# Windowed-attention scores in blocks of 32 queries by 96 keys, from the eleventh token tile on

## The chip, the cores and the metric

The kernel runs on one core of one Trainium2 chip. The metric is the device time of one execution in microseconds (us). The kernel before takes 512.82 us, the median of three runs (511.93 to 513.01).

## What is computed

For 8 sequences of 576 positions and 8 heads of width 64, each query attends to itself and to the 63 positions ahead of it. The result, 4608 tokens by 512 features in fp32, goes through a feed-forward block with a softmax gate and a layer norm.

```python
scores = (q @ k.T) / sqrt(64)
rel = pos[:, None] - pos[None, :]
scores = where((rel >= 0) & (rel < 64), scores, -1e9)
x = softmax(scores) @ v
h = x @ w_in
solu = h * softmax(h)
y = (layer_norm(solu) * g_ln) @ w_out
```

The queries of 32 neighbouring positions need 95 keys between them, those of 64 neighbours need 127.

## The kernel before

The 4608 tokens are cut into 36 tiles of 128, each two blocks of 64 queries of one sequence. One tile goes through these stages.

- `scores` (L445, matmul on L460): for each of 4 pairs of heads, each block of 64 queries (`half`) and each head of the pair (`r`), a matmul of 64 queries by 128 keys with the 64 features of the head as contraction. `r` picks the rows of the TensorE array and `half` its columns, so four such matmuls lie on four array tiles of 64x64. The result goes into a PSUM tile `pS`, where `r` is the outer index. A sequence's first block has no keys ahead of it, and its own keys are read twice. Each fp32 matmul stands in the trace as two records, each with a weight load of its own.
- `softmax` (L468): VectorE adds the mask and takes the maximum out of `pS` (L475, one operation per head, all 128 key columns), ScalarE takes the exponential (L480), GpSimd scales (L498).
- `cross` (L508) and `transposes` (L519): the probabilities are split into 16-bit halves by ScalarE (L512), transposed by DMA (L515, on SP's queue), and joined by VectorE into `PT` (L522).
- `values` (L552, matmul on L559): probabilities times values into `pO`, 32 matmuls of 64 columns a tile, on two array tiles of 128x64; `xH` (L573) and `xL` (L574) are its high and low parts.
- `moe_in` (L585, matmul on L603): 24 matmuls of 512 columns into the one PSUM tile `pH`. `moe_norm` reads `pH` by VectorE (L618), ScalarE (L620) and VectorE (L623), and the next tile's `moe_in` can write it only after L623.
- `moe_cross`, `moe_join` (L666, L669, L679, L683, L685): the normed row is transposed as above, into `yH` and `yL`.
- `moe_out` (L715, matmul on L737): 24 matmuls of 512 columns, and the result is stored.

A planner (`Plan`) writes out the order of every engine. Each step has a cost in ns, its reads and writes and a ring of buffers (`RINGS`; `pS` has 2), and `Plan.order` places the steps by due time and by the costs; the PE order itself is the order in which the steps are written down. The scores of one tile are two steps of cost 480. From the eighth tile on the tiles go in pairs: per pair TensorE runs `values` of two tiles, `scores` of two later tiles, then `moe_out`, `moe_in`, `moe_out`, `moe_in`. `T` (L297) hands out a tile: it makes a new one of the ring for each (tag, number).

Of the kernel before, what the change touches and what calls it, by code (L numbers as in the profile page):

```python
# [18 lines left out]

P = 128  # L20
WIN = 64
BIG = 3.0e38

EXP_HI = 122879.9921875
# [202 lines left out]
def tile_window_attention_solu_moe(  # L227
# [17 lines left out]
    nc = tc.nc  # L245
# [6 lines left out]
    D = P // 2  # L252
# [10 lines left out]
    ps_s = ctx.enter_context(tc.tile_pool(name="ps_s", bufs=1, space=bass.MemoryType.PSUM))  # L263
# [6 lines left out]

    band = const.tile([P, P + WIN], F32, name="band")
    nc.gpsimd.memset(band, 0.0)
    nc.gpsimd.affine_select(
        band, band, pattern=[[-1, P + WIN]], base=WIN, channel_multiplier=1,
        compare_op=ALU.is_ge, fill=NEG)
    nc.gpsimd.affine_select(
        band, band, pattern=[[1, P + WIN]], base=-1, channel_multiplier=-1,
        compare_op=ALU.is_ge, fill=NEG)
    masks = {}
    for first in (0, None, 1):  # L280
        t = masks[first] = const.tile([P, P], F32, name=f"mask{first}")
        nc.gpsimd.tensor_copy(t[:WIN], band[:WIN, :P])
        nc.gpsimd.tensor_copy(t[WIN:], band[WIN:, WIN:])
        if first is not None:
            nc.gpsimd.memset(t[first * WIN:(first + 1) * WIN, :WIN], NEG)

# [7 lines left out]

    plan = Plan(RINGS, NTILE, NW)

    def T(tag, n, shape, dtype=F32, pool=None):  # L297

        if (tag, n) not in plan.tiles:
            plan.tiles[tag, n] = (pool or sb).tile(  # L300
                shape, dtype, tag=tag, name=f"{tag}_{n}", bufs=RINGS[tag])
        return plan.tiles[tag, n]

    def first_of(t):

        return {0: 0, NBLK - 1: 1}.get(2 * t % NBLK)
# [4 lines left out]
    def W32(i):  # L311
        return T("w", i, [P, 2, 512])

    def WL(i):
        return T("w", NW + i, [P, 2, 512], F32R)
# [6 lines left out]
    def weight_block(i, src):  # L322
# [3 lines left out]
        def raw():  # L326
            return T("raw", i, [P, 2, 512, 2], I32)
# [79 lines left out]
    def Q(t):  # L407
        return QK(t)[:, :NPAIR * P].rearrange("d (p s) -> d p s", p=NPAIR)

    def K(t):  # L410
        return QK(t)[:, NPAIR * P:].rearrange("d (p s) -> d p s", p=NPAIR)
# [16 lines left out]
    def SS(t):  # L428
        return T("sS", t, [P, H, P])

    def PS(t, x=0):
        if (t, x) == (0, 1):
            return T("pH", NTILE, [P, 2, NPAIR, P], pool=ps_h)
        return T("pS", t, [P, 2, NPAIR, P], pool=ps_s)

    def S_key(t, x):
        return ("pH", NTILE) if (t, x) == (0, 1) else ("pS", t)
# [7 lines left out]
    def scores(t):  # L445
        first = first_of(t)

        def emit(ps=range(NPAIR)):
            q, k = Q(t), K(t)

            for p in ps:
                for half in range(2):
                    for r in range(2):
                        rs = slice(r * D, (r + 1) * D)
                        keys = k[rs, p, half * WIN:half * WIN + P]
                        if first == half:
                            a = k[rs, p, (half + 1) * WIN:(half + 2) * WIN]
                            keys = bass.AP(
                                tensor=a.tensor, offset=a.offset, ap=[a.ap[0], [0, 2], a.ap[1]])
                        nc.tensor.matmul(  # L460
                            PS(t, p // 2)[half * WIN:(half + 1) * WIN, r, p],
                            q[rs, p, half * WIN:(half + 1) * WIN], keys, start=True, stop=True)

        for x in range(2):
            plan.op("PE", 480, lambda x=x: emit((2 * x, 2 * x + 1)), [("qk", t)], [S_key(t, x)],
                    loose=t < LOOSE)

    def softmax(t):  # L468
        def cols(tag, h):
            return T(tag, t, [P, H], pool=st)[:, h:h + 1]  # L470

        mk = masks[first_of(t)]
        for h in range(H):

            plan.op("DVE", 211, lambda h=h: nc.vector.tensor_tensor_reduce(  # L475
                SS(t)[:, h], PS(t, h // 4)[:, h % 2, h // 2], mk, scale=-SCALE, scalar=BIG,
                op0=ALU.add, op1=ALU.min, accum_out=cols("nmx", h)),
# [283 lines left out]
    def attend(t):  # L761
        on(scores, t + AHEAD)
        on(softmax, t + AHEAD)
        on(cross, t + AHEAD)

    load(0, range(1))
    prep(0)
    scores(0)
    softmax(0)
    load(0, range(1, 2))  # L770
# [3 lines left out]
    transposes(0)  # L774
    values(0)
    scores(1)
    softmax(1)
    prep(3)
# [121 lines left out]
```

## Time and profile before

| what | before |
|---|---|
| median of the runs | 512.82 us (511.93 to 513.01) |
| span of the profiled execution | 510.9 us, first to last instruction; its own time is not listed apart from the runs |
| TensorE (PE) busy | 492.1 us, 96% of the span |
| VectorE (DVE), ScalarE (ACT), GpSimd (POOL) busy | 80%, 70%, 62% |
| score matmuls (L460) | 2 x 576 records, 6% of the chain that ended last |
| granted TensorE clock | full in all 40 slices of the span |

The median of the runs lies 1.9 us above the span, which is what stands around the first and the last instruction. Busy time says where an engine has work, not where it holds the others up; that is read from the chain of waits.

### The profile page before, as it was taken

The page shows a single profiled execution, that of the slowest core. Times are in us where ns is not written, and L with a number is a line of the kernel's source. Part 1 is how long each engine was busy: PE and PEld are TensorE (multiplying, and loading weights), DVE is VectorE, ACT ScalarE, POOL GpSimd, SP SyncE. Part 2 cuts the span into 40 slices and gives each one's busy share as a digit, 9 for nine tenths or more (in the row PEclk, how much of TensorE's full clock was granted, in tenths as well). Part 3 has the DMA queues.
Part 4 walks back from the last instruction along what each step waited for, and adds up shares of the span by engine and source line. Part 5 has one row for each costly group of instructions (what it writes and reads, how often), then busy time and mean ns, then how long its engine had stood idle before and what let it go on. Part 6 is the DMA issues. An engine that isn't in the chain of part 4 may idle for free.

```text
span 510.9 us, 11601 instructions
## 1 busy us (share of the span) xinstructions
PE 492.1 (96%) x4064; PEld 392.4 (77%) x4064; DVE 409.8 (80%) x1176; ACT 355.6 (70%) x960; POOL 314.5 (62%) x566
## 2 busy tenths in 40 slices
PE   2889999999999999999999999999999999999996
PEld 1445577888788888888888888888888888888885
DVE  5998997888796989787978898887878878977531
ACT  4589795868686777777776868686859586865331
POOL 4388467664757475758574858584848485936430
PEclk9999999999999999999999999999999999999999
DMA  8994446966889989898889797879897969764301
GB/s 321 412 410 177 116 120 119 234 156 147 173 219 148 234 164 229 171 223 163 229 151 243 143 250 145 250 141 247 132 244 144 267 117 222 124 131 103 83 21 43
DMA packets 150762, 94.09 MB, mean 184 GB/s; under 512 B 135088, under 2 KB 135344, under 8 KB 150320
## 3 DMA queue, kind: packets, MB, share of 16 engines
q1 hardware_dynamic: 150704, 93.35, 76.7%
q8 instruction: 32, 0.52, 0.5%
q14 instruction: 26, 0.21, 0.1%
HBM read 50.86 MB, written 9.44 MB: 118 GB/s over the span
## 4 chain that ended last, share of the span: by engine, by line
PE 85%; DVE 4%; ACT 2%; POOL 2%; DMA 2%; issue 0%; SPq 0%; ACTq 0%; DVEq 0%; POOLq 0%
PE pH L603 34%; PE pO L737 34%; PE pO L559 6%; PE pS L460 6%; PE pO L724 3%; PE pH L590 1%; DMA raw<-raw 1%; ACT sS L480 1%; POOL sS L498 1%; PE pS L700 1%; DVE e L623 1%; DVE mst L618 1%; DMA y<-ot 1%; ACT e L620 0%; DVE w L368 0%
## 5 line engine op out<-in xcount | busy, mean ns | idle before, releaser
L498 POOL TENSOR_SCALAR sS<-sS,rec 128x128 f32<-128x128 f32 x280 | 149.2, 554 | 10.8 <-PE pS L460 7.4
L480 ACT ACTIVATE sS<-sS,nmx 128x128 f32<-128x128 f32 x288 | 111.5, 389 | 1.5 <-DVE nmx L475 1.4
L737 PE MATMUL pO<-w_outH,yH 128*128 128x512 f32 x272 | 108.2, 398 | 0.0
L737 PE MATMUL pO<-w,yH 128*128 128x512 f32 x272 | 106.1, 390 | 0.0
L603 PE MATMUL pH<-w_inH,xH 128*128 128x512 f32 x264 | 103.7, 393 | 0.8 <-DVE mst L623 0.8
L603 PE MATMUL pH<-w,xH 128*128 128x512 f32 x264 | 101.8, 389 | 0.0
L737 PE MATMUL pO<-w_outH,yL 128*128 128x512 f32 x272 | 83.9, 389 | 0.0
L512 ACT COPY raw<-sS 128x1024 uint16<-128x1024 uint16 x64 | 66.6, 1046 | 22.9 <-POOL sS L498 22.7
L603 PE MATMUL pH<-w_inH,xL 128*128 128x512 f32 x264 | 81.9, 389 | 0.0
L640 POOL TENSOR_SCALAR e<-e,mst 128x512 f32<-128x512 f32 x72 | 66.8, 936 | 3.9
L632 POOL TENSOR_SCALAR mst<-mst 128x1 f32<-128x1 f32 x36 | 19.9, 553 | 79.8 <-ACT sq L629 42.9
L522 DVE COPY PT<-raw 128x1024 uint16<-128x1024 uint16 x64 | 50.0, 789 | 19.9 <-DMA raw<-raw 19.7
L573 ACT CAST xH<-pO 128x512 fp32r<-128x512 f32 x33 | 19.3, 586 | 63.5 <-PE pO L559 63.4
L737 PEld LDWEIGHTS pO<-w_outH,yH 128*128 128x128 f32 x272 | 51.0, 188 | 12.7 <-issue 2.6
L618 DVE TENSOR_REDUCE mst<-pH 128x1 f32<-128x1024 f32 x36 | 44.0, 1221 | 20.1 <-PE pH L603 20.0
L737 PEld LDWEIGHTS pO<-w_outH,yL 128*128 128x128 f32 x272 | 51.1, 188 | 10.9
L603 PEld LDWEIGHTS pH<-w_inH,xH 128*128 128x128 f32 x264 | 49.6, 188 | 12.2 <-PE pO L737 1.2
L737 PEld LDWEIGHTS pO<-w,yH 128*128 128x128 f32 x272 | 51.1, 188 | 10.0
L603 PEld LDWEIGHTS pH<-w_inH,xL 128*128 128x128 f32 x264 | 49.6, 188 | 10.6 <-issue 0.2
L603 PEld LDWEIGHTS pH<-w,xH 128*128 128x128 f32 x264 | 49.6, 188 | 10.4 <-issue 0.2
L626 POOL TENSOR_SCALAR mst<-mst 128x1 f32<-128x1 f32 x36 | 18.9, 524 | 62.3 <-DVE mst L623 56.5
L629 ACT ACTIVATE sq<-e,mst 128x1024 bf16<-128x1024 f32 x36 | 41.4, 1150 | 21.6 <-POOL mst L626 21.6
(71 smaller groups left out, 852.3 us busy)
## 6 DMA issues: line engine op xcount, KB each, us to landing
qk<-qk SPq DMA_DIRECT2D x36, 640.0 KB, 5.9
v<-vS SPq DMA_DIRECT2D x36, 512.0 KB, 4.7
y<-ot SPq DMA_DIRECT2D x35, 256.0 KB, 2.7
raw<-w_out SPq DMA_DIRECT2D x4, 1024.0 KB, 12.0
raw<-w_in SPq DMA_DIRECT2D x3, 1024.0 KB, 11.5
raw<-raw SPq DMA_TRANSPOSE x126, 3.2
raw<-w_in SPq DMA_DIRECT2D x2, 512.0 KB, 6.2
y<-ot SPq DMA_DIRECT2D x2, 128.0 KB, 1.7
```

Source lines behind the costliest of these rows:

```text
L460: nc.tensor.matmul(PS(t, p // 2)[half * WIN:(half + 1) * WIN, r, p], q[rs, p, half * WIN:(half + 1) * WIN], keys, start=True, stop=True)
L480: plan.op("ACT", 390, lambda h=h: nc.scalar.activation(SS(t)[:, h], SS(t)[:, h], AF.Exp, bias=cols("nmx", h), scale=-1.0, accum_out=cols(" ...
L498: plan.op(engine, cost, lambda h=h: v.tensor_scalar(SS(t)[:, h], SS(t)[:, h], rec()[:, h:h + 1], 0.0, ALU.mult, ALU.add), [R], [("sS", t, ...
L512: plan.op("ACT", 1050, lambda x=x: nc.scalar.copy(XP(t)[:, x], SS(t)[:, 4 * x:4 * x + 4].bitcast(U16).rearrange("p h (n w) -> p w (h n)", ...
L522: plan.op("DVE", 740, lambda x=x: nc.vector.tensor_copy(PT(t)[:, 4 * x:4 * x + 4].bitcast(U16).rearrange("p h (n w) -> p h w n", w=2), XP( ...
L559: nc.tensor.matmul(PX(t, p)[r * D:(r + 1) * D, p, ks], V(t, half)[:, h * D:(h + 1) * D], PT(t)[:, h, ks], start=True, stop=True)
L603: plan.op("PE", 235, lambda n=n, c=c, d=d, x=x, w=w: nc.tensor.matmul(PH(t)[:, d * 512:(d + 1) * 512], x(t)[:, c], WH(c, d) if w is WH els ...
L618: plan.op("DVE", 1225, lambda: nc.vector.tensor_reduce(nmax(), PH(t), axis=AX.X, op=ALU.max, negate=True), [("pH", t)], [key(0)])
L629: plan.op("ACT", 1150, lambda: nc.scalar.activation(T("sq", t, [P, DFF], BF16), E(t), AF.Square, bias=nmean(), scale=1.0, accum_out=ss()), ...
L632: plan.op("POOL", 240, lambda: nc.gpsimd.tensor_scalar(kk(), ss(), se(), se(), ALU.mult, ALU.mult), [key(1), key(3)], [key(5)])
L640: plan.op("POOL", 770, lambda h=h, hs=hs: nc.gpsimd.tensor_scalar(E(t)[:, hs], E(t)[:, hs], nmean(), kk(), ALU.add, ALU.mult), [key(4), ke ...
L737: plan.op("PE", 235, lambda n=n, f=f, i=i, x=x, y=y, w=w: nc.tensor.matmul(PO(), y(t)[:, f], w(i, x), start=(n == 0), stop=(n == len(passe ...
```

## The change

From the eleventh tile on (`t >= WHOLE`, tiles 10 to 35 counted from 0) a matmul of the scores holds 32 queries (`s`, four blocks in a tile of 128) and the 96 keys that they can see: half as many weight columns, three quarters of the key columns, and twice the number of matmuls, 32 a tile. `s` picks one of four column groups of the array and `r` one of two row groups, so eight of them lie on eight array tiles of 64x32. Where a sequence begins, the keys ahead of it are left out (32 or 64 columns in place of 96). The other 32 columns of `pS` are not written. So that they hold finite numbers, the two `pS` buffers are made once and kept (`kept`, `turns`), and the first ten tiles are computed whole as before; the mask covers those columns. The planner is told 400 in place of 480 for each of the two steps.

```diff
+QB = 32
+WHOLE = 10
...
+    kept, turns = {}, {}
+
     def T(tag, n, shape, dtype=F32, pool=None):
 
+        if tag == "pS":
+            i = turns.setdefault(n, len(turns)) % 2
+            if i not in kept:
+                kept[i] = ps_s.tile(shape, dtype, name=f"pS{i}_0")
+            return kept[i]
         if (tag, n) not in plan.tiles:
...
             for p in ps:
-                for half in range(2):
+                for half in range(2) if t < WHOLE else ():
                     for r in range(2):
...
+                for s, r in ((s, r) for s in range(4) for r in range(2)) if t >= WHOLE else ():
+                    rs = slice(r * D, (r + 1) * D)
+                    half, o = s // 2, s % 2 * QB
+                    begin = WIN if first == half else o
+                    ks = slice(begin, o + WIN + QB)
+                    nc.tensor.matmul(
+                        PS(t, p // 2)[s * QB:(s + 1) * QB, r, p, ks], q[rs, p, s * QB:(s + 1) * QB],
+                        k[rs, p, half * WIN + ks.start:half * WIN + ks.stop], start=True, stop=True)
+
         for x in range(2):
-            plan.op("PE", 480, lambda x=x: emit((2 * x, 2 * x + 1)), [("qk", t)], [S_key(t, x)],
+            plan.op("PE", 480 if t < WHOLE else 400, lambda x=x: emit((2 * x, 2 * x + 1)), [("qk", t)], [S_key(t, x)],
                     loose=t < LOOSE)
```

The change shifts the line numbers behind it by 9 up to `T`'s end and by 18 after the new loop. On TensorE (PE), the block of scores of the twelfth and thirteenth tile stands so before the change (`pO` is the output of `values` on L559 and of `moe_out` on L737, `qk` the queries and keys of a tile; the size is the output's):

```order
L559 MATMUL pO_1624<-PT_1565,v_1195 64x64 x16
L559 MATMUL pO_1644<-PT_1605,v_1337 64x64 x16
L460 MATMUL pS_1669<-qk_1062 64x128 x16
L460 MATMUL pS_1692<-qk_1383 64x128 x16
L737 MATMUL pO_1712<-w_outH,yH_1550 128x512
L737 MATMUL pO_1712<-w_774,yH_1550 128x512
```

and so with it (L577 is L559 of before, L755 is L737):

```order
L577 MATMUL pO_1624<-PT_1566,v_1181 64x64 x16
L577 MATMUL pO_1644<-PT_1606,v_1323 64x64 x16
L478 MATMUL pS_0_117<-qk_1048 32x96 x32
L478 MATMUL pS_0_181<-qk_1383 32x96 x32
L755 MATMUL pO_1742<-w_outH,yH_1551 128x512
L755 MATMUL pO_1742<-w_765,yH_1551 128x512
```

Sixteen matmuls a tile have become thirty-two smaller ones in the same place; no other row of PE moves anywhere in the program.

On VectorE the new cost moves one step of each pair of tiles: the first join of `y` (L679, L697 now) among the eight softmax steps of a tile. Before:

```order
L679 COPY y_2091<-raw_1991 128x4x2x128
L475 ISA sS_2076,nmx_2077<-pS_2018,maskNone 128x128
L475 ISA nmx_2077 128x1
L475 ISA sS_2076,nmx_2077<-pS_2018,maskNone 128x128
L475 ISA nmx_2077 128x1
L475 ISA sS_2076,nmx_2077<-pS_2018,maskNone 128x128
L475 ISA nmx_2077 128x1
L475 ISA sS_2076,nmx_2077<-pS_2018,maskNone 128x128
L475 ISA nmx_2077 128x1
L493 TENSOR_SCALAR rec_2112<-sm_2063 128x8
```

With the change (L493 is now the softmax, L511 the reciprocal's first step):

```order
L697 COPY y_2155<-raw_2021 128x4x2x128
L493 ISA sS_2138,nmx_2139<-pS_0_181,maskNone 128x128
L493 ISA nmx_2139 128x1
L493 ISA sS_2138,nmx_2139<-pS_0_181,maskNone 128x128
L493 ISA nmx_2139 128x1
L493 ISA sS_2138,nmx_2139<-pS_0_181,maskNone 128x128
L493 ISA nmx_2139 128x1
L511 TENSOR_SCALAR rec_2173<-sm_2125 128x8
```

The join stands one softmax step later here, and two steps later in most of the other pairs. ScalarE, GpSimd and SP keep their order but for a few neighbours, most of them in the last tiles.

## Rows read from the trace of the kernel before

**Rows 1.** The page: busy time of the engines, slices of PE and its granted clock.

```profile
PE 492.1 (96%) x4064; PEld 392.4 (77%) x4064; DVE 409.8 (80%) x1176; ACT 355.6 (70%) x960; POOL 314.5 (62%) x566
...
PE   2889999999999999999999999999999999999996
...
PEclk9999999999999999999999999999999999999999
```

**Rows 2.** Chain that ended last, one pair of tiles: start us, us, what.

```profile
269.68 2.02 PE pO L559 x64
271.70 1.91 PE pS L460 x64
273.61 5.67 PE pO L737 x24
279.28 5.44 PE pH L603 x24
284.72 5.44 PE pO L737 x24
290.16 5.44 PE pH L603 x24
295.60 2.02 PE pO L559 x64
```

**Rows 3.** The same chain at the sixth tile, where tiles still go singly.

```profile
54.01 0.88 PE pS L700 x8
54.89 1.08 PE pO L559 x32
55.97 1.03 PE pS L460 x32
```

**Rows 4.** Instructions of L460, 271.62 to 273.45: count, duration ns min/median/max, first and last start.

```profile
L460 PEld LDWEIGHTS pS<-qk x64: 129/133/133, 271.6 to 273.2; 64*64 64x64 f32 x64
L460 PE MATMUL pS<-qk x64: 269/269/320, 271.6 to 273.3; 64*64 64x128 f32 x64
```

**Rows 5.** L460 in short stretches: length, PE busy (instructions), PEld busy (instructions), clock, DMA.

```profile
271.62:271.66 0.04, 0.03 (x4) 0.03 (x4) 1.00 0.96 359
...
88.46:88.53 0.07, 0.03 (x4) 0.06 (x5) 1.00 0.00 0
```

**Rows 6.** Instructions of L460, 87.2 to 88.6: what PE's sequencer did itself.

```profile
L460 PEldq EVENT_SEMAPHORE  x1: 1176/1176/1176, 87.3 to 87.3; - x1
```

**Rows 7.** Timeline, VectorE around L618 and L623: start us, us, instruction, [idle before].

```profile
258.84 1.23 DVE L618 TENSOR_REDUCE mst<-pH 128x1 f32<-128x1024 f32 x1 [0.65 <-PE pH L603]
...
262.85 0.08 DVE L623 DVE_READ_ACCUMULATOR2_ANT mst<- 128x1 f32 x1
...
285.17 1.21 DVE L618 TENSOR_REDUCE mst<-pH 128x1 f32<-128x1024 f32 x1
...
289.56 0.09 DVE L623 DVE_READ_ACCUMULATOR2_ANT mst<- 128x1 f32 x1
...
185.99 0.08 DVE L623 DVE_READ_ACCUMULATOR2_ANT mst<- 128x1 f32 x1
```

**Rows 8.** Timeline, PE: the first matmul of the `moe_in` behind each of them.

```profile
264.08 0.39 PE L603 MATMUL pH<-w_inH,xH 128*128 128x512 f32 x1
...
290.00 0.39 PE L603 MATMUL pH<-w_inH,xH 128*128 128x512 f32 x1
...
186.22 0.47 PE L603 MATMUL pH<-w_inH,xH 128*128 128x512 f32 x1
```

**Rows 9.** Timeline, VectorE: first softmax of a pair; first join of `y`, a pair earlier.

```profile
274.41 0.28 DVE L475 CUSTOM_DVE_ANT_0 sS<-pS,maskNone 128x128 f32<-128x128 f32 x1
...
251.26 0.76 DVE L679 COPY y<-raw 128x1024 uint16<-128x1024 uint16 x1
```

**Rows 10.** Busy time in one pair of tiles: length, PE, PEld, DVE, ACT, POOL (instructions), clock, DMA share, GB/s.

```profile
295.53:321.44 25.91, 25.91 (x225) 21.62 (x225) 22.49 (x64) 18.95 (x52) 17.37 (x32) 1.00 0.90 198
```

**Rows 11.** The page, DMA queues: packets, MB, share of 16 engines' span.

```profile
q8 instruction: 32, 0.52, 0.5%
```

## The prediction

> **What bounds the kernel now.** [...] In the paired tiles it is PE and nothing else: `values`, `scores`, `moe_out`, `moe_in`, `moe_out`, `moe_in`, and again, 25.92 us a pair (295.60 - 269.68) with no other engine between [rows 2]. A microsecond taken from a PE block there is taken from the span, as long as nothing else becomes late. The block of scores is 1.91 us of the 25.92.
>
> What sets those 1.91 us? A single tile takes 1.03 us and a pair 1.91 [rows 2, 3], so 32 further records cost 0.88 us, and 0.15 us is the change of block. The 32 records are eight groups of four, one on each array tile of 64x64: 110 ns a group. One transpose record of 128 columns on the whole array also takes 110 ns (0.88 us for eight) [rows 3]. So four records lie side by side in the time of one, and what is paid for is the 128 columns that each array tile streams. The start of a group says the same: four loads and four matmuls begin within 0.04 us [rows 5], and then the array is left to stream.
>
> **The change, part by part.**
>
> *Columns.* Per tile there are now 64 records of 96 columns, eight groups of eight in place of eight groups of four. If eight stream side by side as four do, a group costs what 96 columns cost. Two rows bracket that: `values` has 64 columns on two array tiles, 32 further records cost 0.94 us (2.02 - 1.08), which is 59 ns a group of two [rows 2, 3]; 128 columns cost 110 ns. Halfway between lie 96 columns: 84 ns. A group gains 26 ns, a tile 8 x 26 = 0.21 us, a pair 0.42 us. Tiles 10 to 35 are 26, or 13 pairs: 13 x 0.42 = **5.4 us**. The two ends: no column saved in effect (0), or pure proportion, 96/128 of 110 ns = 82.5 ns, 5.7 us. I take 84 ns, as it lies between two rows of the same kind of record. Blocks that begin a sequence have groups with 32 and 64 columns in one half, but the other half still streams 96, so they count alike.
>
> *Weight loads.* They double, to 64 a tile, each of 32 columns where there were 64. In the block they run under the matmuls: 64 loads of 133 ns, 8.5 us in sum, in a block of 1.91 us [rows 2, 4], and none shows in the chain. The first group waits for its load (its record is 320 ns long, the others 269, so 51 ns [rows 4]); with half the columns this shrinks by some 25 ns, while the last group's eight records start further apart than four did, by about as much. I set both to nothing. If the loads lost their cover, a load for 32 columns would at most be half of those 51 ns in each group: 84 + 26 = 110, and the gain would be gone.
>
> *PSUM.* The kept tiles add no wait that is on the path: the softmax of the pair in rows 2 begins only at 274.41, 0.8 us behind its scores, because DVE has `moe_norm` work ahead of it [rows 2, 9], and the next write to the same buffers is a pair later, over 20 us off. Softmax, mask and all later steps have their old sizes.
>
> *The moved join.* It starts one or two softmax steps later, at 0.21 us a step (0.28 us in the trace, overlapping); its result is needed by the second `moe_out`, which begins 7 us behind it (at 284.72 less one pair, 258.80) [rows 2, 9]. Cost: nothing. If its load were late, it would hold up the softmax steps behind it by a few tenths.
>
> *What becomes late next.* PE has no slack, so look at who feeds it just in time. The `moe_in` behind the second `moe_out` needs `pH` free: L623 ends at 262.93 and the matmul starts at 264.08, 1.15 us spare; DVE had even idled 0.65 us for PE ahead of that chain [rows 7, 8]. At 290.00 the spare time is 0.35 us, with DVE late for L618, and at 186.22 it is 0.15 us [rows 7, 8]. Taking 0.42 us from PE in such a pair takes it from the spare time: 0.27 us comes back as a wait at 186 and 0.07 at 290. The other pairs of this trace have 0.45 us or more, and DVE's 22.49 us of work fit a pair of 25.5 us [rows 10]. Cost: **0.3 us**. Bounds: 0, and 13 x 0.42 if every pair were held.
>
> *Instruction fetch.* PE's instructions arrive in pieces of 0.52 MB / 32 = 16 KB, 256 instructions of 64 bytes (8128 loads and matmuls make 0.52 MB) [rows 1, 11]. A fetch keeps a DMA engine 0.005 x 16 x 510.9 / 32 = 1.3 us. A pair now issues 576 instructions in place of 448, and 384 of them, not 256, in the `values` and `scores` blocks; 256 instructions of the new score block last 16 x 84 = 1.34 us, about as long as one fetch. Nothing stalls there now (each block is 2.02 and 1.91 us) [rows 2]. A whole piece lies within the dense stretch in (384 - 256) / 256, half of the pairs; bounds 0 and 6.5 x 1.3 = 8.5 us. I take **0.5 us**, near the lower end, since a fetch can start a piece ahead.
>
> Sum: 5.4 - 0.3 - 0.5 = 4.6 us off the span, 510.9 to 506.3. The median lies 1.9 us above the span of the profiled execution, so **508.2 us**. A measurement of this kernel tells some 0.2%, 1.0 us, from no change.
>
> **The rivals.**
>
> *Instructions come too slowly (slower, or no gain).* The old block issues 8 instructions per 110 ns, 13.8 ns each; the new one needs 16 in 84 ns, 5.3 ns each. No stretch of this trace sustains that. For it: if 13.8 ns were the limit, a group would take 220 ns and the block 16 x 110 ns more, 13 x 1.76 = 22.9 us in all: 535.7 us. Against it: after PE's sequencer had itself waited 1176 ns [rows 6], so that nothing could be queued, five loads and four matmuls started within 0.07 us [rows 5], 7.8 ns each or less. At 7.8 ns a group takes 125 ns and the time is 512.8 + 13 x 16 x 0.015 = 515.9 us. It decides from 110 / 16 = 6.9 ns an instruction: below, part of the gain stays (0 to 4.6 us); above, the change is slower. [...] Chances: gain cut but left, 509.5 to 512.5 us, 0.12; slower, 514 to 536 us, 0.10.
>
> *Four column groups don't stream side by side.* No row shows more than two column groups at once. If the array's inputs carried two and then two, a group would take 168 ns: 13 x 16 x 0.058 = 12.1 us more, 524.9 us. Against it: with one column group or two, on whole rows or half rows, the price follows the columns alone [rows 2, 3]. [...] Chance 0.08.
>
> *The gain is taken back downstream.* PE runs ahead, and `pH`, the transposing DMAs (share 0.90 [rows 10]) or instruction fetches hold it in most pairs. By the bounds above, 512.8 less 0 to 1.5: 511.3 to 513 us. Chance 0.08.
>
> **How the numbers follow.** The forecast, 506.8 to 509.5 us, has 0.62. All of it is faster, as are 0.10 of the cut gain and 0.03 of the gain taken back: 0.75. Within 0.2%: 0.02 + 0.05 + 0.01 of the slow supply near its turning point, 0.08. Slower: the rest, 0.17. The range from 506.8 (all columns in proportion, no loss: 512.8 - 5.7, and a little for run to run) to 512.8 takes in the forecast, the cut gain and the gain taken back, and leaves 0.18 above it.
>
> **What would show it.** Right: the pair's period falls from 25.92 to about 25.5 us, the block of scores from 1.91 to about 1.5 us, its 128 records in groups of eight, and PE still unbroken from 160 to 488 us but for a wait on L623 here and there. A block near 1.75 us or more means that instructions come too slowly; near 2.8, that column groups take turns. A block of 1.5 us with new gaps ahead of `moe_in` or `values` means that the gain was taken back, and the engine named there says by whom. The forecast is wrong if the block isn't shorter.

## The result and the profile after

The changed kernel is slower.

| | before | after |
|---|---|---|
| median of the timed runs, us | 512.51 (511.93 to 513.01, 4 runs) | 520.16 (519.06 to 521.88, 4 runs) |
| ratio, 95% interval | | 1.0148 (1.0127 to 1.0170) |
| span of the profiled execution, us | 510.9 | 518.3 |

The forecast was 508.2 us with a range from 506.8 to 512.8, so it is wrong in sign. Line numbers moved by 18 below the scores: in the rows from here on `values` is L577, `moe_in` L621, `moe_out` L755, the old score form L469 and the new one L478.

The page of the changed kernel, busy time, slices and the instruction queue:

```profile
PE 491.3 (95%) x4896; PEld 391.0 (75%) x4896; DVE 404.9 (78%) x1176; ACT 355.7 (69%) x960; POOL 310.5 (60%) x566
...
PE   2789999999989999999998999999999999999997
...
PEclk9999999999989999999999999999999999999999
...
q8 instruction: 38, 0.62, 0.5%
```

PE's busy time is 0.8 us below that of before, yet the span is 7.4 us longer [rows 1]. So the new time is idle PE, and past the start two slices of PE and one of its clock show an 8. The instruction queue moved 38 pieces where it had moved 32 [rows 11].

The chain that ended last in the changed kernel (start us, us, what; `x` counts records, of which overlapping ones are left out):

```profile
139.17 2.02 PE pO L577 x64
141.18 1.65 PE pS L478 x97
142.83 1.67 issue
144.50 0.36 PE pS L478 x4
144.86 7.28 PE pO L755 x24
...
168.45 2.02 PE pO L577 x64
170.47 1.25 PE pS L478 x53
171.72 0.83 issue
172.54 0.74 PE pS L478 x37
...
195.31 2.02 PE pO L577 x64
197.32 1.70 PE pS L478 x102
199.02 5.67 PE pO L755 x24
...
221.01 2.02 PE pO L577 x64
...
434.44 1.66 PE pS L478 x100
436.10 2.72 PE pO L755 x11
438.82 0.29 issue
439.11 3.13 PE pO L755 x13
...
458.56 2.02 PE pO L577 x64
```

"issue" is PE waiting for nothing that the profile shows: no semaphore, no buffer. Of the twelve blocks of scores of a whole pair in the steady stretch, six have such a hole (the first, second, fifth, sixth, ninth and tenth), and behind the twelfth it falls into `moe_out`. The period is the distance between two starts of L577: 29.28 us (168.45 - 139.17) and 26.86 us with a hole, 25.70 us without (221.01 - 195.31), against 25.92 before [rows 2]. The waits of the whole span say the same in one row:

```profile
PE pS L478 <- issue: 7.3, 6, 1.7
```

An undisturbed block takes 1.70 us, 0.21 less than before, where 0.42 was forecast. The first hole costs twice. Stretches behind it (length, PE, PEld, DVE, ACT and POOL busy, granted clock, DMA share, GB/s):

```profile
144.79:151.97 7.18, 7.18 (x26) 5.75 (x25) 6.24 (x38) 7.18 (x35) 5.12 (x7) 0.76 0.80 153
151.97:168.38 16.41, 16.41 (x73) 13.32 (x71) 9.60 (x17) 9.16 (x14) 10.18 (x23) 1.00 0.72 151
```

PE had stood still from 142.6 to 144.5 us; for 3.4 of the next 7.18 us (145.9 to 149.3) its granted clock was 0.50 of the full level (mean 0.76 over the stretch), and the `moe_out` there took 7.28 us in place of 5.67.

The sum, from the chain: from the first L577 above to the one at 458.56 lie twelve pairs in 319.39 us; twelve periods of before are 311.0. Of the 8.4 us, five pairs without a hole gave back 0.2 each (-1.0), six pairs with a hole in the scores cost +7.6 (their periods less 25.92, without the lower clock), the lower clock 1.6 and the hole in `moe_out` 0.2, net of the shorter block.

### The profile page after: what moved, and what is told of

It reads as the page before. It is cut to its first block, busy times and chain, and to the rows that moved or that the text cites. A ratio compares the mean times of both kernels' runs of the same rounds, so it can differ in the third digit from the quotient of the medians.

```text
span 518.3 us, 13261 instructions
## 1 busy us (share of the span) xinstructions
PE 491.3 (95%) x4896; PEld 391.0 (75%) x4896; DVE 404.9 (78%) x1176; ACT 355.7 (69%) x960; POOL 310.5 (60%) x566
## 4 chain that ended last, share of the span: by engine, by line
PE 84%; DVE 3%; POOL 2%; ACT 2%; issue 2%; DMA 2%; ACTq 0%; DVEq 0%; POOLq 0%
PE pO L755 34%; PE pH L621 34%; PE pO L577 6%; PE pS L478 4%; PE pO L742 3%; DMA raw<-raw 2%; PE pH L608 1%; POOL sS L516 1%; PE pS L718 1%; PE pS L469 1%; ACT sS L498 1%; DVE yL L729 1%; DVE y L697 1%; DVE e L641 0%; DVE mst L636 0%
## 5 line engine op out<-in xcount | busy, mean ns | idle before, releaser
L516 POOL TENSOR_SCALAR sS<-sS,rec 128x128 f32<-128x128 f32 x280 | 141.0, 522 | 9.4 <-PE pS L469 7.4
L755 PE MATMUL pO<-w_outH,yH 128*128 128x512 f32 x272 | 108.7, 400 | 0.0
L755 PE MATMUL pO<-w,yH 128*128 128x512 f32 x272 | 106.5, 392 | 0.0
L621 PE MATMUL pH<-w_inH,xH 128*128 128x512 f32 x264 | 103.6, 393 | 0.3 <-DVE mst L641 0.3
L621 PE MATMUL pH<-w,xH 128*128 128x512 f32 x264 | 101.8, 389 | 0.0
L755 PE MATMUL pO<-w_outH,yL 128*128 128x512 f32 x272 | 84.8, 393 | 0.3 <-issue 0.3
L621 PE MATMUL pH<-w_inH,xL 128*128 128x512 f32 x264 | 81.9, 389 | 0.0
L658 POOL TENSOR_SCALAR e<-e,mst 128x512 f32<-128x512 f32 x72 | 71.0, 995 | 3.9
L650 POOL TENSOR_SCALAR mst<-mst 128x1 f32<-128x1 f32 x36 | 19.1, 531 | 82.3 <-ACT sq L647 47.2
L591 ACT CAST xH<-pO 128x512 fp32r<-128x512 f32 x33 | 19.3, 586 | 68.0 <-PE pO L577 67.9
L644 POOL TENSOR_SCALAR mst<-mst 128x1 f32<-128x1 f32 x36 | 18.0, 500 | 73.2 <-DVE mst L641 56.7
L755 PEld LDWEIGHTS pO<-w_outH,yH 128*128 128x128 f32 x272 | 51.5, 189 | 12.9 <-ACT sS L498 0.5
L755 PEld LDWEIGHTS pO<-w_outH,yL 128*128 128x128 f32 x272 | 51.5, 189 | 11.0
L755 PEld LDWEIGHTS pO<-w,yH 128*128 128x128 f32 x272 | 51.4, 189 | 10.2
L621 PEld LDWEIGHTS pH<-w_inH,xH 128*128 128x128 f32 x264 | 49.6, 188 | 11.4 <-PE pO L755 0.7
L621 PEld LDWEIGHTS pH<-w_inH,xL 128*128 128x128 f32 x264 | 49.5, 188 | 10.5 <-issue 0.2
L621 PEld LDWEIGHTS pH<-w,xH 128*128 128x128 f32 x264 | 49.6, 188 | 10.5 <-issue 0.2
```

The source lines that it names most:

```text
L516: plan.op(engine, cost, lambda h=h: v.tensor_scalar(SS(t)[:, h], SS(t)[:, h], rec()[:, h:h + 1], 0.0, ALU.mult, ALU.add), [R], [("sS", t, ...
L591: plan.op("ACT", 560, lambda: nc.scalar.copy(XH(t), PX(t)), [("pO", NTILE + t)], [("xH", t)])
L621: plan.op("PE", 235, lambda n=n, c=c, d=d, x=x, w=w: nc.tensor.matmul(PH(t)[:, d * 512:(d + 1) * 512], x(t)[:, c], WH(c, d) if w is WH els ...
L658: plan.op("POOL", 770, lambda h=h, hs=hs: nc.gpsimd.tensor_scalar(E(t)[:, hs], E(t)[:, hs], nmean(), kk(), ALU.add, ALU.mult), [key(4), ke ...
L755: plan.op("PE", 235, lambda n=n, f=f, i=i, x=x, y=y, w=w: nc.tensor.matmul(PO(), y(t)[:, f], w(i, x), start=(n == 0), stop=(n == len(passe ...
```

## The experiments

**Where the holes stand.** Numbering PE's instructions (loads, matmuls and the few semaphore instructions) in time order shows it: every hole is at an instruction whose number is 193 modulo 256 (2497, 3009, 4801, 5313, 7105, 7617, 8897). The view of busy time shows the distances. Stretches from the end of one hole to the end of the next:

```profile
144.50:172.54 28.04, 27.21 (x254) 22.27 (x255) 20.18 (x62) 18.80 (x52) 15.78 (x29) 0.94 0.76 171
172.54:251.45 78.91, 77.79 (x892) 64.77 (x891) 64.90 (x195) 57.01 (x157) 50.34 (x91) 1.00 0.90 193
251.45:278.33 26.88, 25.58 (x254) 21.11 (x255) 21.01 (x65) 18.89 (x52) 16.73 (x30) 1.00 0.85 187
```

254 matmuls, 255 loads and 3 semaphore instructions are 512; 892, 891 and 9 (three pairs) are 1792, which is 7 x 256. That is the size of the pieces in which instructions arrive: the page has 9792 loads and matmuls of PE and 38 transfers on q8, 258 to each. And in the first hole such a piece is just arriving: the DMA queues between 142.20 and 143.16 us, whose end is 1.34 us before PE goes on, have it.

```profile
q8 instruction: 1, 0.02, 6.3%
```

The same row stands for 170.27 to 171.23 us, 1.31 us before PE goes on behind the second hole at 172.54. The whole record has this pattern. From the paired tiles on PE stops 27 times at such a number, in the change and the runs below, and each time it goes on 1.2 to 1.5 us after the end of one 16 KB transfer on q8. In the change the seven transfers begin 0.8 to 2.3 us after PE passed the boundary before (the number that is 256 lower) and take 0.9 to 1.0 us. Where PE came to a boundary later than that after the end of the transfer (2.0 us and more in the change), it did not stop.

My theory for the runs: when a whole piece of 256 instructions lies in the dense stretch of `values` and `scores` (the 384 instructions of a pair that follow each other at this pace, 2.02 + 1.70 = 3.72 us), PE has gone through it before the next piece is there. The rivals: the kept PSUM tiles or the new order; column groups that take turns (the array serving two of the four at a time); the form itself, wherever it stands.

**The kept tiles and the order alone.** The new form is left out, all else of the change stays:

```diff
-                for half in range(2) if t < WHOLE else ():
+                for half in range(2):
...
-                for s, r in ((s, r) for s in range(4) for r in range(2)) if t >= WHOLE else ():
+                for s, r in ():
```

> All scores in the old 64x128 matmuls, with the two kept PSUM tiles and the planner's 400 left in. If the loss comes from the pieces in which PE's instructions are fetched, or from the rate at which they are issued: 512.5 us, the same as before within 1 us, score blocks of 1.91 us a pair and no gap of over 1 us in them. If the kept tiles or the moved VectorE steps cost the time: 517 to 521 us.

Measured: 512.57 us, ratio 1.0007 (0.9994 to 1.0019). The blocks in its chain are those of before, without a hole:

```profile
271.23 1.91 PE pS L469 x64
```

Kept tiles, the moved join and the planner's price cost nothing that shows. The loss comes with the new form.

**The same kernel, 128 instructions later.** Tile 6 computes its scores three times, which moves every later instruction by half a piece:

```diff
-... lambda x=x: emit((2 * x, 2 * x + 1)), ...
+... lambda x=x: emit((2 * x, 2 * x + 1) * (3 if t == 6 else 1)), ...
```

> The change, with the scores of the seventh tile computed three times (same result, 128 more instructions on PE, about 1.7 us). Fetch theory: every gap in PE's stream still stands at the same instruction number modulo 256 (193 in the profile of the change), so the gaps move to other pairs: of the thirteen score blocks from the twelfth tile on, numbers 3, 4, 7, 8, 11 and 12 have one of 0.6 to 1.9 us (1, 2, 4, 5, 8 and 9 in the change), 10 perhaps a short one; time 518 to 523 us. If a DMA of q and k or a semaphore makes the gaps: they stay in blocks 1, 2, 4, 5, 8 and 9.

Measured: 518.64 us in one run. The expectation names the change's blocks with a hole as 1, 2, 4, 5, 8 and 9; counted in its chain they are 1, 2, 5, 6, 9 and 10. The new chain, the first block that lost its hole and the first that got one:

```profile
143.36 1.66 PE pS L478 x100
145.01 5.68 PE pO L755 x24
...
194.91 1.59 PE pS L478 x98
196.50 1.12 issue
197.62 0.37 PE pS L478 x7
```

The holes moved from blocks 1, 2, 5, 6, 9 and 10 to blocks 3, 4, 7, 8 and 11, again at numbers that are 193 modulo 256 (3777, 4289, 6081, 6593, 8385). A twelfth block was expected to have one and had none, although PE went through its whole piece in 2.52 us (431.16 to 433.68): that piece began only 24 instructions into the dense stretch, and the transfer for the next one had begun at 429.06, 2.1 us before PE reached it. So the short piece did not stall PE here, where the next transfer had started early. Kernel text, tiles and data around the blocks are the same in both runs; the holes went with the instruction number.

**Half the heads in the old form.** Heads with odd `p` in the old form, so that a pair issues 320 dense instructions, not 384, with forms alternating:

```diff
-                for half in range(2) if t < WHOLE else ():
+                for half in range(2) if t < WHOLE or p % 2 else ():
...
-                for s, r in ((s, r) for s in range(4) for r in range(2)) if t >= WHOLE else ():
+                for s, r in ((s, r) for s in range(4) for r in range(2)) if t >= WHOLE and not p % 2 else ():
```

> From the eleventh tile on, two of the four head pairs in the new form, two in the old. A pair of tiles then issues 515 instructions, 3 off two pieces of 256, so the boundary of a piece stands 152 to 116 instructions into each dense stretch of 320, and no piece lies in it whole. Fetch theory: no gap of over 0.3 us in any score block. Issue theory (8.25 ns an instruction once PE's queue is drained, so new groups at 82 ns only while it is full): blocks of 1.65 to 1.75 us, 13 x 0.2 = 2.6 us under before, 509.5 to 510.5 us. If the columns of new groups streamed by turns or the gaps came from the new shape as such: gaps in about half of the blocks, or blocks of 2.3 us or more, 513 to 518 us.

Measured: 524.05 us, ratio 1.0220 (1.0195 to 1.0245). No hole is left in any block, as fetch would have it (a mild test, as the blocks became longer), but it is the slowest kernel of all and far from the 509.5 to 510.5 us of the expectation. In its chain a block falls into pieces:

```profile
196.58 0.33 PE pS L478 x16
196.91 0.38 PE pS L469 x8
197.28 0.33 PE pS L478 x16
197.61 0.38 PE pS L469 x8
```

Two groups of the new form should take 2 x 82.5 ns and two of the old one 2 x 110 ns, 0.385 us together; they take 0.71. Each change between array tiles of 64x32 and 64x64 cost some 0.16 us here (half of 0.71 - 0.385), and a pair has eight such stretches, four of each form: its block takes 2.8 us in place of 1.91.

**Full width, same instructions.** 32 queries by all 128 key columns (a sequence's first block reads its own keys twice again; the cut end of the last line has this):

```diff
-                    ks = slice(begin, o + WIN + QB)
...
-                        PS(t, p // 2)[s * QB:(s + 1) * QB, r, p, ks], ...
+                        PS(t, p // 2)[s * QB:(s + 1) * QB, r, p], ...
```

> The change with 128 key columns in each matmul of 32 queries, as many instructions. Issue theory: groups of eight go from 82 ns (queue full) or about 106 ns (queue drained) to 110 ns throughout, the pair's block without a gap from 1.70 to about 1.93 us, the gaps in the same blocks and a little shorter, 519 to 522 us. If column groups took turns: 2 x 110 ns a group, blocks of 3.6 us and more, 535 us or over.

Measured: 522.52 us in one run. An undisturbed block in its chain (L481 there) takes 1.96 us, and holes stand at the same six numbers. They were expected to be a little shorter; the one in the fifth block is longer, 2.7 us from start to start, where the transfer on q8 took 2.5 us (248.62 to 251.09) in place of 1. The undisturbed block:

```profile
196.38 1.96 PE pS L481 x128
```

Sixteen groups of 109 ns and a change of block: four column groups side by side cost what their columns cost, and taking turns (3.6 us or more at this width) is out. It also shows that twice as many loads and matmuls add only 0.05 us to the block when each has 128 columns.

**Half the columns.** Why is the block 1.70 us and not 1.49? The block with 48 columns a matmul, which leaves out about half of the scores:

```diff
-                    ks = slice(begin, o + WIN + QB)
+                    ks = slice(max(begin, o + QB + QB // 2), o + WIN + QB)
```

> The change with the matmuls of the score blocks cut from 96 key columns to the last 48 (those with 32 and 64 columns become 16 and 48 or stay as they are); it leaves out about half of the scores. Instruction count and their places in the 256-instruction pieces stay the same. Theory: once PE's queue is drained, an ungapped score block is paced by the instructions themselves (16.5 ns for a load and its matmul, 8.25 ns for each), so fewer columns change little: ungapped block 1.55 to 1.70 us (now 1.70 to 1.71), and the gaps stand at the same instruction numbers (2497, 3009, 4801, 5313, 7105, 7617). Rival, columns pace the block (80 ns for eight matmuls of 96): the block falls to about 0.85 to 1.1 us. Rival, the gaps come of something in the tiles' data or columns: they shift or go.

Measured: 518.62 us in one run; undisturbed blocks of 1.42 to 1.47 us, outside both expectations (1.55 to 1.70, or 0.85 to 1.1). The holes stay at the same six numbers and at 8897, so they don't come of the columns or the data.

```profile
197.18 1.44 PE pS L478 x89
```

The starts of the first record of each group of eight tell more. In the change's block at 197.25 us they are 107, 82, 83, 82, 131, 88, 82, 83, 135, 88, 86, 82, 83, 97 and 104 ns apart: most groups are paced by their 96 columns (82.5 ns), and some are 5 to 50 ns longer, 0.18 us in all (1413 ns less 15 x 82.5). With 48 columns the first five are 67, 47, 42, 99 and 131 ns, and six of the ten behind them 66 to 68, the others 82 to 184: columns would allow 41, so there it is the instructions that pace, 16 in 66 ns or 4.1 ns each. My expectation of 8.25 ns an instruction was wrong, but so was pure column pace. That the supply of instructions also lengthens the single groups at 96 columns fits this, but was not shown; what holds them was not tried.

**Values and scores apart.** The scores of a pair are put ahead of the `moe_in` that stood before `values`, so no dense stretch is longer than 256 instructions:

```diff
-        for u in ss:
+        for u in ss if not late else ():
             scores(u)
...
+            if t > PAIRS + 1 and even:
+                on(scores, t + AHEAD + LEAD)
+                on(scores, t + AHEAD + LEAD + 1)
             on(moe_in, t, 1)
```

> The change with the score block of a pair put ahead of the moe_in block that precedes its values block, so that the 128 instructions of the values and the 256 of the scores no longer follow each other: a dense stretch is at most 256 instructions, as before the change. Theory, fetch of 256-instruction pieces against dense stretches: no gap inside a score block, ungapped blocks of 1.70 us; against before that is 13 x -0.2 us, plus one more switch of tiling in each pair of about 0.2 to 0.35 us (what the row before each values block shows: 0.317 us from the last full matmul to the first load), so 511 to 514 us. Rival, a block of scores in this form draws gaps wherever it stands: gaps of 1.1 to 1.9 us in six of twelve blocks stay, 519 to 522 us.

Measured: 521.73 us, ratio 1.0180 (1.0163 to 1.0197). Its twelve blocks of a pair take 1.60 to 1.68 us and none has a hole: the form alone draws none. The time was still 8 us above the expected 511 to 514, through a wait that I had not counted. The chain of one pair:

```profile
346.87 1.62 PE pS L478 x86
348.49 5.71 PE pH L621 x24
354.20 1.10 PE pO L577 x32
355.33 0.59 ACT xH L591
355.95 0.70 DVE xL L592
356.69 5.74 PE pO L755 x24
```

`moe_out` behind `values` now waits until its PSUM is read by L591 and L592 (8.3 us in 14 waits over the span), which the scores used to cover. So in the kernel before, the scores between `values` and `moe_out` hide that wait; this is what their place there is worth.

**The form only where a piece boundary is harmless.** Behind a pair in the new form the boundary lies 67 instructions nearer to the start of the next dense stretch, behind one in the old form 61 farther from it (185, 118, 179, 112 in this kernel). So the pairs can be chosen by counting:

```diff
-WHOLE = 10
+FINE = (11, 12, 15, 16, 19, 20, 23, 24, 27, 28)
...
-                for half in range(2) if t < WHOLE else ():
+                for half in range(2) if t not in FINE else ():
...
-                for s, r in ((s, r) for s in range(4) for r in range(2)) if t >= WHOLE else ():
+                for s, r in ((s, r) for s in range(4) for r in range(2)) if t in FINE else ():
...
-            plan.op("PE", 480 if t < WHOLE else 400, ...
+            plan.op("PE", 480 if t not in FINE else 400, ...
```

> The new form only in tiles 11, 12, 15, 16, 19, 20, 23, 24, 27 and 28 (every other pair), the old form in all other tiles, chosen by counting instructions: in these pairs the 256-instruction boundary lies 155 or more instructions into the dense stretch of 384 (185, 179, 173, 167, 161), where the change showed no gap, and in the others the stretch is 256 long. Theory: no gap in any block, five blocks of 1.70 instead of 1.91 us, 512.5 - 5 x 0.2 = 511.5 us (511.2 to 512.0). Rival, gaps follow the form and not the boundary: gaps in about half of the five blocks, 1.1 to 1.9 us each, and a fall of the clock, 515 to 518 us.

Measured: 512.98 us, ratio 1.0001 (0.9989 to 1.0013); the 1.0 us gain did not come. The blocks did what they should (five of 1.64 to 1.72 us, no hole in them). Two things took it back, in its chain:

```profile
350.41 3.85 PE pO L755 x16
354.26 0.23 issue
354.49 2.11 PE pO L755 x8
...
454.16 0.61 DVE xL L592
```

In the fifth chosen pair a boundary at 161 lets the end of the whole piece fall 32 instructions into `moe_out` (16 loads, 16 matmuls), too early still; the start there comes 0.4 us late. In the fourth, with 38 instructions of `moe_out` ahead of it, the piece is 0.2 us late as well, and in the three runs below it is not: the chosen places leave little room. And at the last single tile PE waits 0.6 us for L592. With the planner's 400 in these tiles alone VectorE has another order of work than before, so I tried the same without it.

**Four pairs, the old order.** The fifth pair goes back to the old form and the planner's price stays at 480, which leaves every other engine exactly in the order of before:

```diff
-FINE = (11, 12, 15, 16, 19, 20, 23, 24, 27, 28)
+FINE = (11, 12, 15, 16, 19, 20, 23, 24)
...
-            plan.op("PE", 480 if t not in FINE else 400, ...
+            plan.op("PE", 480, ...
```

> As in the run with five chosen pairs, but the new form only in tiles 11, 12, 15, 16, 19, 20, 23 and 24 (boundaries 185, 179, 173 and 167 instructions into the dense stretch) and the planner's price of the score block left at 480 everywhere, which gives every other engine exactly the order of the kernel before. Theory: four blocks of 1.70 instead of 1.91 us, no gap, and no wait at the last single tile (the 0.6 us of the five-pair run came of the other order on VectorE): 0.8 us faster than before, ratio 0.998 to 0.9995. Rival, the time that the shorter blocks save is waited for elsewhere whatever the order: PE waits of 0.6 us or more appear behind them and the ratio is 1.000 or more.

Measured: 511.39 us, ratio 0.9966 (0.9954 to 0.9977). No hole, no wait at the end, blocks of 1.72 us; but more than the blocks explain. (The order and the fifth pair changed together here, so which of them brought the wait at the end was not told apart.) So it ran once more:

> The run with four chosen pairs once more, as it came out faster (ratio 0.9966, interval 0.9954 to 0.9977) than four blocks of 0.2 us explain. If the blocks are all there is, the ratio is 0.998 to 0.999 (four shorter blocks 0.8 us, and the wait of 0.3 us that the trace before shows ahead of one pair); if it is 0.9955 to 0.9975 again, something else in this kernel is faster and stays open.

Measured: 511.83 us, ratio 0.9982 (0.9970 to 0.9994), what the blocks give. The larger figure was not found again; the two intervals overlap.

**Six pairs.** Two later pairs whose boundaries lie far enough back:

```diff
-FINE = (11, 12, 15, 16, 19, 20, 23, 24)
+FINE = (11, 12, 15, 16, 19, 20, 23, 24, 29, 30, 33, 34)
```

> As the run with four chosen pairs, with tiles 29, 30, 33 and 34 in the new form too: by the count of instructions their boundaries lie 222 and 216 into the dense stretch, where the change showed no gap (242, 230, 218), while 27, 28 at 161 stay in the old form. Theory: six blocks of 1.70 us, no gap, 0.4 us less than with four; against before 1.2 us, ratio 0.9965 to 0.9985. Rival, the late pairs wait for the softmax of the last tile: a wait of 0.6 us or more there, no gain over four.

Measured: 511.29 us, ratio 0.9964 (0.9950 to 0.9978): faster than both kernels, by 1.8 us than before (0.0036 x 512.56; 1.1 to 2.6 by the interval; the medians, 512.56 and 511.29, lie 1.3 apart), where 1.2 was expected. That it beats the four pairs is not shown, as the intervals overlap. In its chain the block that had the change's longest hole and a late one:

```profile
141.87 1.71 PE pS L478 x104
143.58 5.69 PE pO L755 x24
...
374.34 1.66 PE pS L478 x101
376.00 5.67 PE pO L755 x24
```

## Why the prediction was wrong

*What bounds the kernel* was right: PE alone in the paired stretch. A hole in PE of 1 us is 1 us of time, which is also why it lost.

*Instruction fetch* is the term that failed: "I take 0.5 us, near the lower end, since a fetch can start a piece ahead." The mechanism and its count stood there, a whole piece inside the dense stretch in half of the pairs, and 6.5 of 13 was right: six blocks and one `moe_out`. The size was not. The six holes in the blocks cost 7.6 us net, and the lower clock behind the first one 1.6 us that no bound held. That the 7.6 lie under the bound of 8.5 is luck: the bound priced a stall at the 1.3 us for which a fetch keeps a DMA engine, and five of the six are longer from start to start (1.3 to 1.9 us).

What failed in it is the head start. In the change the transfer that PE then waits for begins 0.8 to 2.3 us after PE has passed the boundary before, and 1.2 to 1.4 us go by from its end until PE goes on. So not 1.3 us but all this time has to be covered by the piece: behind a dense stretch's first boundary PE goes on at the second 3.2 to 4.1 us later (for the second block, 169.14 and 172.54). "Nothing stalls there now" was true and no argument: the 256 instructions of the old dense stretch last 3.93 us [rows 2], but no boundary stood at its start, and by the same count no piece of the kernel before lasted less than 5.4 us. The change made the dense stretch 384 instructions long, so that half of the stretches hold a whole piece.

Over the span of the change 31 of the 38 pieces show no wait; the seven of the dense stretches do. Why some transfers begin before PE passes the boundary before (311.56 us, 4.7 us ahead) and others after it (176.96 us, 4.4 us behind) stays open.

*Columns* went half wrong: 84 ns a group is right for most groups (82.5), and the block with 128 columns keeps 109. But some groups in each block are 5 to 50 ns longer, so the pair gains 0.21 and not 0.42 us: 13 x 0.21 = 2.7 us in place of 5.4. The rival "instructions come too slowly" had a gain cut but left among its outcomes, at 0.12, which is what the blocks without a hole show; its limit of 7.8 ns an instruction was too high, as six groups of the run with 48 columns went at 4.1. That 520.16 us lies in this rival's range for "slower" (514 to 536, chance 0.10) does not bear it out, as the time went into holes and not into slow groups. For the same reason the sign "near 2.8, that column groups take turns" would have misled: the second block takes 1.25 + 0.83 + 0.74 = 2.82 us, but with a hole in it.

*Weight loads*: right. With full columns the doubled loads add 0.05 us to a block.

*PSUM* and *the moved join*: right, 1.0007 with these alone.

*What becomes late next*: 0.3 us was expected in waits of `moe_in` on what was L623 (now L641). None of 0.1 us or more came in the paired tiles (160 to 488 us), neither in the change, where holes gave VectorE time, nor in the kernel with six pairs. The only such wait is ahead of the `moe_in` at 133 us: 0.3 us in the change, 0.8 in the kernel before, none to 0.6 in the runs with chosen pairs. The spare time of 0.15 us at 186.22 was also misread. That `moe_in` had already waited for L623 in the kernel before, and the 0.15 us are the handover from VectorE to PE, as long as at 134.16, where the trace names L623 as what PE waited for:

```profile
186.23 5.71 PE pH L603 x24
```

It takes 5.71 us in place of 5.44 there.

*Column groups side by side*: the rival of turns is refuted by 1.96 us for 128 columns.

With the terms as measured the sum reads 512.8 + 7.6 (six holes, net of the gain of their blocks) + 1.6 (lower clock) + 0.2 (hole in `moe_out`, net) - 1.0 (the five blocks without a hole) = 521.2 us, where 520.16 was measured. Most of the 1.0 us between them shows in the chains of the two profiled executions: the changed kernel reaches the first of the twelve pairs 0.7 us earlier (139.17 against 139.84), and one pair of the kernel before, the one with the `moe_in` at 186.23, is 0.3 us longer than the 25.92 that the sum takes.

## What to carry to other kernels

Count instructions as well as time: when a tuning step splits work into more and shorter instructions, find the shortest time in which the engine goes through a piece of them (256 for PE here), from boundary to boundary, and treat a piece that may get shorter than any in the trace before (5.4 us here) as a stall like those of 1.1 to 1.9 us here until a run shows otherwise. The rows of the instruction queue say when the next piece comes. Idle time that the chain puts down to "issue", at a fixed distance in instructions (multiples of 256 here), was the sign of it, and its place was moved by moving the count by 128, not only by undoing the change. Small work between two large blocks may be hiding a wait of its neighbour (8.3 us in 14 waits came out here), so moving it is not free even when its own time is unchanged.

## What the runs showed of the hardware

- PE stalled at the end of a piece of 256 instructions when the next one came late: in all 27 stalls it went on 1.2 to 1.5 us after the end of a transfer on q8. With the whole piece in the dense stretch the steps from start to start took 1.1 to 1.9 us in the change (0.9 to 2.7 in all runs), with one exception, where the transfer began early and a piece of 2.52 us went by without a stall. With values and scores apart one of 2.20 us did (399.69 to 401.89), with a transfer that ended at 397.31.
- Where the piece ended 23 to 38 instructions behind the dense stretch, in `moe_out`, PE was late by 0.8 us or less, or not at all, at one and the same place too: at 23 it was 0.4, 0.02 and 0.8 us (the change, 128 and 48 columns). A placement by count alone does not settle these.
- After the first stall of the change (1.9 us) the granted clock was 0.50 of its full level for 3.4 us, which cost 1.6 us of time, and likewise it was 0.76 in the mean from 144.72 to 151.90 in the run with 48 columns; in the run with 128 columns a stall of 2.7 us in the fifth block had no such effect (1.00 from 252.61 to 259.00), so the length of the stall alone doesn't decide it.
- Changing between array tiles of 64x64 and 64x32 cost about 0.16 us each time (half the heads in the old form: 0.71 us in place of 0.385 for two changes), as much as two groups of the small tiles' work.
- Eight array tiles of 64x32 streamed side by side: 82.5 ns for eight matmuls of 96 columns, 109 ns for 128. At 48 columns a load and its matmul went in 8.2 ns, the fastest pace seen over a whole group here but for the first groups of a block (42 ns for eight).
